# Second pair one batch at a time, and loads in a gated order, in a feature-map attention with an MLP

## The chip, the cores and the metric

The kernel runs on one core of a Trainium2 chip. A core has five engines with an instruction queue each, which run in order and wait for each other by semaphores: PE (TensorE, matmuls; its weight loads are shown as PEld), DVE (VectorE), ACT (ScalarE), POOL (GpSimd) and SP (SyncE, which here only issues DMAs). Sixteen DMA engines move the data. PE reads its operands from SBUF, the on-chip memory, and writes to PSUM, which has eight banks. The metric is the device time of one execution in microseconds (us), as the median of several runs. A profile of one execution gives the details.

## The reference

Attention with a feature map in place of the softmax, for 8 batches of 8 heads, 576 tokens, 64 channels per head and 128 features; then a layer norm and an MLP with a residual on the 512 joined channels.

```python
def phi(x):
    proj = einsum('bhsd,df->bhsf', x, w_phi)
    proj = proj - max(abs(proj), axis=-1, keepdims=True)
    return concatenate([exp(proj), exp(-proj)], axis=-1)
q_p, k_p = phi(q), phi(k)
kv  = einsum('bhsf,bhsd->bhfd', k_p, v)
z   = sum(k_p, axis=2)
num = einsum('bhsf,bhfd->bhsd', q_p, kv)
den = einsum('bhsf,bhf->bhs', q_p, z)[..., None] + 1e-06
x   = (num / den), heads joined: (8, 576, 512)
xn  = (x - mu) / sqrt(var + 1e-06) * g_ln
out = x + maximum(xn @ w_ch1, 0.0) @ w_ch2          # 512 -> 2048 -> 512
```

All of it is given and returned in float32. The kernel multiplies in bfloat16 and accumulates in float32.

## The kernel before, in words

The eight batches are worked in four pairs (`NPAIR`). One unit is two heads of 576 tokens; a pair has 8 units, so there are 32, numbered n = 0 to 31. A unit's 1152 token rows are eight full tiles of 128 rows and one mixed tile with the last 64 rows of both heads. `heads` says which two heads form a unit. In pair 0 they are two neighbouring heads of one batch, so that units 0 to 3 finish batch 0 and units 4 to 7 batch 1. In pairs 1 to 3 they are the same head of both batches, so that neither batch is finished before the eighth unit is.

**Steps of a unit.** The keys and queries are turned so that channels lie on partitions: on PE in pair 0 (`a_trans`, L485 and L493), and by a cast (`a_trans_dma`, L545 on DVE, L547 on ACT or L549 on POOL) and a transposing DMA on SP (L568) from unit 8 on. `a_mixed` (L590 to L607) treats the mixed tile. `a_k` multiplies the keys with `w_phi` (L632), takes the maxima on DVE (L638), the exponentials on ACT (L648), and scales the values on POOL into `vv` (`scale_main`, L659, L664 and L668). `a_q` and `a_tails` (units 0 to 3, L708 and L751) or `a_qt` (later units, L784 and L789) do the same for the queries, in both layouts. `a_kv` (L838, L843) sums key features times values over all tokens; `a_num` (L887, L893) multiplies with the query features, and DVE (L902, L907, L911) and POOL (L917) divide and put the result into `x`. In pair 0 each half unit's result goes to `x` in two pieces per head, and the mixed rows of the other half go through a buffer `xs` and a small DMA (L976).

**The MLP.** `x_stats` and `x_center` (L1034, L1049, L1053 or L1058) prepare the norm of each tile of `x`; the centered tiles are turned on PE in pair 0 (`x_trans`, L997) and by DMA later (`x_trans_dma`, L1021). `BLOCKS` groups the nine tiles of a pair: (0,2), (2,4), (4,6), (6,9) in pair 0, and three blocks of three tiles in the others. `moe_block` multiplies a block with `w1` (L1120, 16 groups of four matmuls), applies the ReLU on DVE or ACT (L1128, L1130), multiplies the previous block with `w2` (L1150), and adds `x` (L1157) before the store (L1082, L1091). Pair 0 has `g_ln` folded in when `x` is turned; from pair 1 on it is folded into `w1`, which DVE scales in place (`scale_w1`, L467, 16 operations) when pair 1's first block is due.

**Loads.** One DMA on SP brings one operand of one unit (256 KB), `load_tails` the mixed rows of four units in two DMAs of 64 KB. The order is: batch 0's, then those of units 4 and 5, 6 and 7, and later ones at their due times. `w1` (four blocks of 1 MB in float32, cast on the way) is issued by POOL (L440) once the second query has come, and `w2` (L451) once all of `w1` has.

**The order of the work.** No engine's order is written by hand. Every step is added to the class `Order` with its engines, an estimated time, what it reads and writes, the PSUM banks it takes (pool A: 2, B: 3, N: 1) and a rank. `backward` gives each step a latest start, counted back from the MLP's due times; to it an offset is added, from the table `OFF`, by the kind of step and one of three ranges of units (0 to 3, 4 to 7, later: `stage_table`). `run` plays the engines forward and gives each free engine the ready step of lowest rank. Where the plan has PE idle before `WARM` (36 us of the plan), it inserts filler matmuls on a zero tile `wz` (L1347), to keep PE's clock up. Each engine then gets its steps in the planned order, and on the chip they only wait for semaphores. `RING` (60) is the amount of outstanding DMA above which the plan holds an issuing queue back. Steps marked `port` get longer in the plan while POOL is busy, by 1.0 us at most.

Of the kernel before, what the change touches and what calls it, by code (L numbers as in the profile page):

```python
# [17 lines left out]
def bcast(ap: bass.AP, dim: int, n: int) -> bass.AP:  # L18
# [9 lines left out]
OFF = (  # L28
    {
        "en": 0, "gln": 404.4, "k": 731.6, "k.copy": 69.4, "k.em": -232.2, "k.exp": 2503.5,  # L30
        "k.max": 95, "k.trans": 40.9, "kv": 899.6, "kv.copy": -103, "ln": 482.7, "mixed": 18.6,
        "mixed.exp": -123.6, "mixed.max": 174.2, "num0": -2477.8, "num0.dve": -58.1,
        "num0.put": 178.6, "num1": 209.2, "num1.dve": 318.7, "num1.put": -457.6, "q.copy": -276.1,
        "q.trans": -426.8, "q0": -1263.9, "q0.em": 149.7, "q0.max": 0, "q1": -821.5,
        "q1.em": -990.6, "q1.max": -13.6, "tails0": -719.9, "tails0.exp": -90.7, "tails1": -225.7,
        "tails1.exp": 0, "vv": 215.8, "w2": 3061.6, "x.copy": -132.9, "x.trans": -1573.1,
    },
    {
        "en": 1225.8, "k": -596.1, "k.copy": 123.9, "k.em": 639.7, "k.exp": 9.2, "k.max": 81.3,
        "k.trans": -90.1, "kv": 0, "kv.copy": -360, "ln": 262.7, "load": 0, "mixed": -1206,  # L40
        "mixed.exp": -223.1, "mixed.max": 1308.1, "num0": 517.5, "num0.dve": -73.3,
        "num0.put": 141.8, "num1": 67.4, "num1.dve": -802.1, "num1.put": 0, "q.copy": -784.4,
        "q.em": 5.6, "q.max": 36.6, "q.trans": 753.5, "qt": -360.9, "rstd": -179.5,
        "tails.exp": 199, "vv": 2452.3, "x.copy": 195.6, "x.trans": -942.9,
    },
    {
        "en": 167.8, "k": 108.9, "k.em": 424.2, "k.exp": -788, "k.max": 25.2, "kv": -30.9,
        "kv.copy": 8.3, "ln": 12.2, "load": 1357.4, "mixed": -2096, "mixed.exp": 54.6,
        "mixed.max": 4.8, "num0": -162.6, "num0.dve": -161.9, "num0.put": -15.2, "num1": -692.4,
        "num1.dve": -457.5, "num1.put": -223.9, "q.em": -210.7, "q.max": -16.1, "qt": -860.5,  # L50
        "rstd": 81.2, "tails.exp": -53.9, "trans": 253.4, "vv": 2822.4, "w1": 1149.9,
    },
)
# [9 lines left out]
class Order:  # L63

    ENGINES = ("PE", "DVE", "ACT", "POOL", "SP")
    START, LAND, RING, TURN, COLD = 1.15, 0.75, 60.0, 0.095, 5.5
# [36 lines left out]
    def run(self):  # L103
# [21 lines left out]
        while True:  # L125
# [30 lines left out]
            for engine in self.ENGINES:  # L156
# [4 lines left out]
                while queue:  # L161
                    item = heapq.heappop(queue)
                    op = item[2]
                    if op.engine:
                        op = None
                        continue
                    full = op.dma and out.get(op.dma[0], 0.0) > self.RING
                    if not full and all(room[res] >= n for res, n in op.acquire):
                        break
                    passed.append(item)  # L170
                    op = None
# [18 lines left out]
                elif engine == "DVE" and op.port:  # L190
                    us += min(max(free["POOL"] - now, 0.0), 1.0)
# [22 lines left out]
def kernel(  # L214
# [44 lines left out]
    EARLY, NUMB, TILED = 4, 0, 4  # L259
# [40 lines left out]
    for i in range(2):  # L300
# [3 lines left out]
        nc.gpsimd.memset(vx, 0.0)  # L304
        nc.gpsimd.memset(vx[0:64, :, 0, D:D1], 1.0)
        nc.gpsimd.memset(vx[64:128, :, 1, D:D1], 1.0)
# [7 lines left out]
    for i in range(EXB):  # L314
        ex = consts.tile([P, 2, 2 * P], BF16, name=f"ex{i}")
        nc.gpsimd.memset(ex, 0.0)
        ex_bufs.append(ex)

    w1_sb = consts.tile([P, KC, DH], BF16, name="w1")
    w2_sb = consts.tile([P, JC, DM], BF16, name="w2")  # L320

# [40 lines left out]
    def issue(queue, rank, dst, src, keys, nbytes, row=1024):  # L362
        eng = nc.sync if queue == "SP" else nc.scalar
        dma(
            queue, rank, nbytes / row, lambda: eng.dma_start(out=dst, in_=src), w=keys,
            us=0.65 if row == 256 else 0.52, ns=0.019 if row == 256 else 0.045,
        )

    def heads(pair, i, half):

        if pair == 0:
            return i // 4, 2 * (i % 4) + half, 2
        return 2 * pair + half, i, 1

    def load_main(key, n, nu, rank, queue):
# [7 lines left out]
        if pair == 0:  # L383
# [9 lines left out]
                262144 * nu,  # L393
            )
            return
        for half in range(2):
# [7 lines left out]
                [(key + str(half), g % NBUF, u) for u in us], 131072 * nu,  # L404
            )

    def load_tails(key, n, rank, queue):
# [4 lines left out]
        for half in range(2):  # L412
# [9 lines left out]
            issue(queue, rank, dst, src, [(key + "x" + str(half), j)], 16384 * TG, row=256)  # L422
# [25 lines left out]
    def load_w2(n, V):  # L448
# [9 lines left out]
        dma("POOL", V, 512, emit, r=[("w1 came", NW - 1)], w=[("w2", n)], us=0.75, ns=0.094)  # L458

    def scale_w1(n, rank):  # L460
# [5 lines left out]
        def scale(kc):  # L466
            nc.vector.tensor_scalar(  # L467
                out=w1_sb[:, kc, sl], in0=w1_sb[:, kc, sl], scalar1=gln_sb[:, kc : kc + 1],
                scalar2=-1.0, op0=ALU.mult, op1=ALU.mult,
            )  # L470

        for kc in range(KC):
            add("DVE", 0.3, rank, lambda kc=kc: scale(kc), r=["gln"], w=[("w1", n, kc)])
# [63 lines left out]
    def a_trans_dma(u):  # L537
# [28 lines left out]
        def turn():  # L566
# [6 lines left out]
        add(("DVE", "ACT", "POOL"), (0.12, 0.19, 0.8), rank, cast_mixed,  # L573
# [5 lines left out]
            us=1.3, ns=0.019)  # L579

    def a_mixed(u):
# [11 lines left out]
        def maxima():  # L593
            nc.vector.reduce_max(
                out=u["m"][:, :, u["mx"]],
# [28 lines left out]
    def a_k(u):  # L624
# [17 lines left out]
        def em():  # L642
            t_ = u["em", 1]
            e = u["mx"] + 1
# [7 lines left out]
        def en():  # L652
            e = u["mx"] + 1
            nc.scalar.activation(u["en"][:, 0:e], u["m"][:, 1, 0:e], AF.Exp, scale=-1.0)

        def scale_main(t):
            vb, vx = v_bufs[u["g"] % NBUF], vx_bufs[n // TG % 2]
# [5 lines left out]
            )  # L663
            nc.gpsimd.tensor_copy(  # L664
# [5 lines left out]
                in1=bcast(bcast(e[:, u["mx"] : u["mx"] + 1], 1, 2), 3, D1), op=ALU.mult,  # L670
# [14 lines left out]
        for t, e in ((1, ("em", 1, n % NEM)), (0, ("en", n % NEM))):  # L685
            add("POOL", 1.5, rk("vv", n), lambda t=t: scale_main(t),
                r=[e, *vdata] + [("vv", 1, n % VVB)] * (1 - t), w=[("vv", t, n % VVB)])

    def q_part(u, s):

        qT = u["qkT"][:, 0:512]
        if s is None:
            return qT.rearrange("p (c t) -> p c t", t=P)
        return qT.rearrange("p (h s t) -> p s h t", h=2, s=2)[:, s]

    def a_q(u, s=None):

        n = u["n"]
        x = "" if s is None else str(s)
        nc_ = 4 if s is None else 2  # L700

        def products():
            shape = [P, 2 * nc_, F]
            pool, tag = (ps_A, "A") if s is None else (ps_B, "B")
            u["pq", s] = ps = pool.tile(shape, FP32, tag=tag, name="pq")
            chunks = q_part(u, s)
            for c in range(nc_):
# [4 lines left out]
        def maxima():  # L712
            m, ps = u["m"][:, 0, :], u["pq", s]
            if s is not None:
                out = m[:, 6 * s : 6 * s + 4]
            elif u["pair"]:
                out = m[:, 0:MX]
            else:
                out = m.rearrange("p (s r) -> p s r", s=2)[:, :, 0:4].rearrange(
                    "p s (h a) -> p h s a", h=2  # L720
                )
                ps = ps.rearrange("p (h s a) f -> p h s a f", h=2, s=2)
            nc.vector.reduce_max(out=out, in_=ps, axis=AX.X, apply_absolute_value=True)

        def em():
            lo, hi = {None: (0, u["mx"] + 1), 0: (0, 4), 1: (6, u["mx"] + 1)}[s]
# [4 lines left out]
        parts = (0, 1) if s is None else (s,)  # L731
        room = [("A" if s is None else "B", 1)]
        mk = [("m", 0, p, n % NEM) for p in parts]
        add("PE", mm(nc_, 256), rk("q" + x, n), products, r=[("qkT", n % QB, 0), ("T", n % QB, 0)],
            w=[("pq", s, n)], acquire=room)
# [649 lines left out]
```

## Time and profile before

| what | value |
|---|---|
| median of 6 runs | 385.44 us (383.11 to 386.6) |
| the profiled execution | 385.26 us |
| its span, first to last instruction | 383.5 us |
| mean granted PE clock | 0.989 |
| HBM read, written | 36.77 MB, 9.44 MB |
| DMA, mean over the span | 139 GB/s |
| PE's matmuls L1120, L1150 (the MLP), busy | 154.2 us, 144.5 us |
| PE's fillers L1347, busy | 24.1 us, x309 |

The profile gives, for each engine, the busy time and, for groups of instructions by line, the count, the mean duration and the idle time of the engine just before them with what ended it. Busy times of groups that overlap on PE add up to more than the engine's. A line of a timeline gives the start and the duration in us, the engine, the line of the kernel, the operation with its tiles, and in brackets the idle time before it. A line of windows gives a stretch of the run, its length, the busy time of PE, PEld, DVE, ACT and POOL with the number of instructions, the granted PE clock (1 is full), the DMA engines' busy share and the GB/s moved. Idle time of an engine that doesn't set the end costs nothing.

### The profile page before, as it was taken

To read this page: it belongs to the slowest core of one execution; us is meant where nothing else is said; L and a number is where in the kernel's file an instruction comes from. 1 tells how busy PE (TensorE), PEld (TensorE's weight loads), DVE (VectorE), ACT (ScalarE), POOL (GpSimd) and SP (SyncE) were. 2 spreads that over 40 slices of the span, in tenths; PEclk is the share of its full clock that TensorE was granted. 3 is DMA by queue.
4 is the path that set the end of the run, shared out by engine and by line. 5 is a ranking of instruction groups with operands and counts; after the bars stand their busy time and mean duration, and the time that the engine had idled before them with its cause. 6 is when DMAs were issued, how large, how long until landed. Compare 5 with 4: busy or idle time off the path is not lost.

```text
span 383.5 us, 9303 instructions
## 1 busy us (share of the span) xinstructions
PE 361.4 (94%) x3516; PEld 232.7 (61%) x3562; DVE 297.9 (78%) x633; ACT 226.5 (59%) x539; POOL 181.7 (47%) x334
## 2 busy tenths in 40 slices
PE   7999689998996999999999999999999999999995
PEld 6999567665763555656566656566665555555543
DVE  4789999996997899978987899788878745454532
ACT  3999997778975678786786777867643300000000
POOL 4958968976657666164655751654451000000000
PEclk9999999998998999999999999999999999999999
DMA  7999799799999674968452547310010530110102
GB/s 201 256 239 325 156 259 166 200 281 248 231 215 290 159 225 98 257 131 213 91 134 45 127 115 163 75 30 30 18 40 27 111 89 34 30 55 29 46 37 85
DMA packets 92589, 53.31 MB, mean 139 GB/s; under 512 B 59008, under 2 KB 88064, under 8 KB 92544
## 3 DMA queue, kind: packets, MB, share of 16 engines
q1 hardware_dynamic: 86944, 48.18, 49.3%
q0 software_dynamic: 4224, 4.19, 6.7%
q8 instruction: 28, 0.46, 0.5%
q10 hardware_dynamic: 1376, 0.33, 0.4%
q14 instruction: 17, 0.14, 0.1%
HBM read 36.77 MB, written 9.44 MB: 120 GB/s over the span
## 4 chain that ended last, share of the span: by engine, by line
PE 63%; DVE 12%; DMA 12%; POOL 6%; issue 3%; ACT 2%; SPq 1%; DVEq 0%; POOLq 0%; ACTq 0%
PE hT_ps L1120 25%; PE ch_ps L1150 23%; DMA qk<-in_k_dram 4%; PE n_bank L843 3%; DMA qkT<-b 3%; PE pk L632 2%; DVE w L467 2%; POOL vv L659 2%; PE n_bank L1347 2%; PE num L887 2%; DVE hT L1128 2%; DVE m L638 1%; PE pq L784 1%; POOL x L917 1%; DMA xT<-xc 1%
## 5 line engine op out<-in xcount | busy, mean ns | idle before, releaser
L1120 PE MATMUL hT_ps<-xT,w 128*128 128x384 bf16 (+1 forms) x832 | 154.2, 315 | 1.0 <-ACT xT L1009 0.3
L1150 PE MATMUL ch_ps<-w,hT 128*128 128x512 bf16 (+1 forms) x546 | 144.5, 376 | 4.0 <-ACT xT L1009 2.1
L1120 PEld LDWEIGHTS <-w 128*128 128x128 bf16 x832 | 77.8, 98 | 54.4 <-issue 4.9
L1128 DVE TENSOR_SCALAR hT<-hT_ps 128x384 bf16<-128x384 f32 (+1 forms) x136 | 71.4, 525 | 47.9 <-PE hT_ps L1120 46.0
L1150 PEld LDWEIGHTS <-hT 128*128 128x128 bf16 x592 | 54.7, 98 | 42.9 <-issue 3.7
L659 POOL TENSOR_TENSOR vv<-v,em 128x512 bf16<-128x512 f32 x64 | 67.7, 1058 | 24.4 <-ACT em L645 16.0
L917 POOL TENSOR_TENSOR x<-numc,rden 128x384 bf16<-128x384 f32 (+3 forms) x88 | 45.9, 536 | 66.5 <-DVE rden L911 64.5
L1130 ACT ACTIVATE hT<-hT_ps 128x384 bf16<-128x384 f32 (+1 forms) x72 | 33.3, 466 | 68.2 <-PE hT_ps L1120 67.8
L648 ACT ACTIVATE eb<-pk 128x1024 bf16<-128x1024 f32 x64 | 65.6, 1041 | 5.1 <-DVE m L638 5.0
L810 ACT ACTIVATE ea<-pt 128x1024 bf16<-128x1024 f32 x56 | 57.0, 1028 | 15.6 <-PE pt L789 15.1
L638 DVE TENSOR_REDUCE m<-pk 128x8 f32<-128x1024 f32 x32 | 38.8, 1214 | 5.1 <-PE pk L632 5.0
L803 DVE TENSOR_REDUCE m<-pq 128x8 f32<-128x1024 f32 x28 | 33.9, 1210 | 1.0 <-PE pq L784 1.0
L1157 DVE SCALAR_TENSOR_TENSOR o<-ch_ps,rstd,x 128x512 f32<-128x512 f32 (+1 forms) x37 | 26.9, 728 | 9.1 <-PE ch_ps L1150 7.9
L887 PEld LDWEIGHTS <-ea 128*128 128x128 bf16 x512 | 25.6, 99 | 8.0 <-issue 1.9
L843 PE MATMUL n_bank<-vv,eb 128*128 128x65 bf16 x512 | 26.9, 194 | 0.0
L843 PEld LDWEIGHTS <-eb 128*128 128x128 bf16 x512 | 22.3, 98 | 7.0 <-issue 4.1
L632 PE MATMUL pk<-wbk,qkT 128*128 128x256 bf16 x128 | 20.0, 281 | 6.7 <-DVE m L803 5.4
L549 POOL TENSOR_TENSOR b<-qk,one 128x1024 bf16<-128x1024 f32 x11 | 21.1, 1915 | 10.9 <-DMA qkT<-b 10.9
L668 POOL TENSOR_TENSOR vv<-vx,em 128x130 bf16<-128x130 f32 x64 | 26.1, 409 | 0.0
L1034 DVE BATCH_NORM_STATS2 st<-x 128x6 f32<-128x512 bf16 (+1 forms) x44 | 24.5, 582 | 0.7 <-POOL x L917 0.5
L1347 PE MATMUL n_bank<-wz 128*128 128x120 bf16 x309 | 24.1, 229 | 0.4 <-DVE KV L850 0.4
L902 DVE TENSOR_TENSOR numc<-num,em 128x390 f32<-128x390 f32 (+2 forms) x40 | 20.6, 514 | 1.7 <-PE num L887 0.5
(89 smaller groups left out, 446.3 us busy)
## 6 DMA issues: line engine op xcount, KB each, us to landing
qk<-in_k_dram SPq DMA_DIRECT2D x32, 256.0 KB, 4.0
v<-in_v_dram SPq DMA_DIRECT2D x32, 256.0 KB, 3.8
qk<-in_q_dram SPq DMA_DIRECT2D x32, 256.0 KB, 5.1
out_dram<-o SPq DMA_DIRECT2D x31, 256.0 KB, 2.6
w<-in_moe_w_ch_dram POOLq DMA_DIRECT2D x8, 512.0 KB, 9.3
out_dram<-o SPq DMA_DIRECT2D x9, 128.0 KB, 2.5
qx<-in_k_dram SPq DMA_DIRECT2D x16, 64.0 KB, 4.2
vx<-in_v_dram SPq DMA_DIRECT2D x16, 64.0 KB, 3.8
```

The costliest lines, as they stand in the source:

```text
L638: nc.vector.reduce_max(out=u["m"][:, 1, 0:MX], in_=u["pk"], axis=AX.X, apply_absolute_value=True)
L648: nc.scalar.activation(u["EB"][:, t, 0:MX, :], u["pk"], AF.Exp, scale=(1.0, -1.0)[t])
L659: nc.gpsimd.tensor_tensor(out=u["vv"][:, t, 0:MX, 0:D], in0=vb[:, hh, :].rearrange("p (c d) -> p c d", d=D), in1=bcast(e[:, 0:MX], 2, D), ...
L803: nc.vector.reduce_max(out=out, in_=ps, axis=AX.X, apply_absolute_value=True)
L810: nc.scalar.activation(u["EA"][:, t, :], u["pt", None], AF.Exp, scale=(1.0, -1.0)[t])
L843: nc.tensor.matmul(ps[:, t, c // 4, :], EB[:, t, c, :], vv[:, t, c, :], start=False, stop=(t == 0 and c == MX - 1), skip_group_check=True,)
L887: nc.tensor.matmul(ps[t][:, i, :], ea(u, t, c), KV[:, t, c // 4, :], start=True, stop=True,)
L917: nc.gpsimd.tensor_tensor(out=dst, in0=st["numc"][ps_, i : i + n, 0:D], in1=bcast(st["rden"][ps_, i : i + n], 2, D), op=ALU.mult,)
L1120: nc.tensor.matmul(st["ps"], w1_sb[:, kc, jj * P : (jj + 1) * P], xT_bufs[xj][:, kc : nt * KC : KC, :], start=(kc == 0), stop=(kc == KC - 1),)
L1128: nc.vector.tensor_relu(h_sb[:, 0 : nt * P], st["ps"])
L1130: nc.scalar.activation(h_sb[:, 0 : nt * P], st["ps"], AF.Relu)
L1150: nc.tensor.matmul(ch[t, c][:, cols], hT[jj][:, rt * P : (rt + 1) * P], w2_sb[:, jj, cols], start=(jj == 0), stop=(jj == JC - 1),)
```

## The change

- **Pair 1 by batches.** `SPLIT = 2`: units 8 to 11 are batch 2 and units 12 to 15 batch 3, as in pair 0. The query maxima now lie in tile order, without gaps. `a_num` puts a unit's result in two pieces per head in pair 1 too, and its mixed rows go through `xs`. `x_stats` works on half rows for pair 1's full tiles. `BLOCKS` is unchanged, so pair 1's first block (tiles 0 to 2) needs batch 2 alone, the second (tiles 3 to 5) both batches.
- **Loads.** SP gets two gates, tiny DMAs that read a piece of a weight block and so wait for it: one on the third block of `w1`, ahead of batch 1's loads, and one on the third block of `w2`, ahead of all loads from unit 8 on. `w2` waits for the query of unit 7 to have come (before: for the last block of `w1`). Units 8 to 15 are loaded two at a time, 512 KB in one DMA.
- **Memsets.** Those of the `vx` and `ex` buffers move from POOL to DVE.
- **vv in two steps.** The scaling of the full tiles no longer waits for the mixed rows; these and the column of ones are a step of their own on POOL.
- **scale_w1** multiplies with the negated scale alone and may run on DVE or ACT.
- **The order model.** `RING` is 128 and counts the DMA to be issued; DVE's wait for POOL has no upper limit; some estimates change; `OFF` has a value for each of the units 0 to 11, for units 12 to 15 and for each later pair. All engines' orders are new.

```diff
-    START, LAND, RING, TURN, COLD = 1.15, 0.75, 60.0, 0.095, 5.5
+    START, LAND, RING, TURN, COLD = 1.15, 0.75, 128.0, 0.095, 5.5
...
-                    full = op.dma and out.get(op.dma[0], 0.0) > self.RING
+                    full = op.dma and out.get(op.dma[0], 0.0) + op.dma[1] > self.RING
...
-                    us += min(max(free["POOL"] - now, 0.0), 1.0)
+                    us += max(free["POOL"] - now, 0.0)
...
-    EARLY, NUMB, TILED = 4, 0, 4
+    EARLY, SPLIT, GATE = 4, 2, 2
...
-        nc.gpsimd.memset(vx, 0.0)
-        nc.gpsimd.memset(vx[0:64, :, 0, D:D1], 1.0)
-        nc.gpsimd.memset(vx[64:128, :, 1, D:D1], 1.0)
+        nc.vector.memset(vx, 0.0)
+        nc.vector.memset(vx[0:64, :, 0, D:D1], 1.0)
+        nc.vector.memset(vx[64:128, :, 1, D:D1], 1.0)
...
-        nc.gpsimd.memset(ex, 0.0)
+        nc.vector.memset(ex, 0.0)
...
+    def gate_of(n):
+        return None if n < H // 2 else "w1" if n < H else "w2"
+
+    def gate(key, n):
+        src = w1_sb[0:1, 0, n * WC : n * WC + 8] if key == "w1" else w2_sb[0:1, n * JC // NW, 0:8]
+        add(
+            "SP", 0.6, rk("load", 0), lambda: nc.sync.dma_start(out=seen, in_=src),
+            r=[("w1", n, 0) if key == "w1" else ("w2", n)], w=[("gate", key)], lag=0.0,
+        )
+
     def heads(pair, i, half):
-        if pair == 0:
-            return i // 4, 2 * (i % 4) + half, 2
+        if pair < SPLIT:
+            return 2 * pair + i // 4, 2 * (i % 4) + half, 2
         return 2 * pair + half, i, 1
...
-        dma("POOL", V, 512, emit, r=[("w1 came", NW - 1)], w=[("w2", n)], us=0.75, ns=0.094)
+        dma("POOL", V, 512, emit, r=gate, w=[("w2", n)], us=0.75, ns=0.094)
...
-        def scale(kc):
-            nc.vector.tensor_scalar(
-                out=w1_sb[:, kc, sl], in0=w1_sb[:, kc, sl], scalar1=gln_sb[:, kc : kc + 1],
-                scalar2=-1.0, op0=ALU.mult, op1=ALU.mult,
-            )
+        def scale(kc, engine):
+            w, g = w1_sb[:, kc, sl], ngln[:, kc : kc + 1]
+            if engine == "DVE":
+                nc.vector.tensor_scalar_mul(out=w, in0=w, scalar1=g)
+            else:
+                nc.scalar.activation(w, w, AF.Copy, scale=g)
...
-            add("POOL", 1.5, rk("vv", n), lambda t=t: scale_main(t),
-                r=[e, *vdata] + [("vv", 1, n % VVB)] * (1 - t), w=[("vv", t, n % VVB)])
+            add("POOL", 1.0, rk("vv", n), lambda t=t: scale_main(t),
+                r=[e, *vdata[0:2]] + [("vv", 1, n % VVB)] * (1 - t), w=[("vv", t, n % VVB)])
+            add("POOL", 0.5, rk("vv", n), lambda t=t: scale_rest(t),
+                r=[e, *vdata[2:4]] + [("vvx", 1, n % VVB)] * (1 - t), w=[("vvx", t, n % VVB)])
...
-        if pair:
+        if not split:
             h = u["h"]
...
-            t0, ht = 4 * b + 2 * part, 2
+            ht = min(nt, MX - lo) // 2
+            t0 = 4 * b + lo // 2
...
-        split = pair == 0 and t < MX
+        split = pair < SPLIT and t < MX
...
-        return (n >= H // 2) + (n >= H)
+        return n if n < 12 else 11 + n // 8
...
-    add("POOL", 4.6, -999.0, None)
+    add("POOL", 1.8, -999.0, None)
-    add("DVE", 1.3, -999.0, None)
+    add("DVE", 3.0, -999.0, None)
...
-    for key in "kqv":
-        load_tails(key, 4, next(rank), "SP")
+    gate("w1", NW - 2)
     for n in (4, 5):
-        for key in "kvq":
-            load_main(key, n, 1, next(rank), "SP")
-    for n in range(NW):
-        load_w2(n, rk("w2", 0))
+        if n == 4:
+            for key in "kqv":
+                load_main(key, 4, 1, next(rank), "SP")
+                load_tails(key, 4, next(rank), "SP")
+        else:
+            for key in "kvq":
+                load_main(key, n, 1, next(rank), "SP")
...
+            if n == 1:
+                for j in range(NW):
+                    load_w2(j, rk("w2", 0), [("came", "q", 7)])
+                gate("w2", GATE)
...
-            if w["pair"] == 0:
+            if w["pair"] < SPLIT:
                 tiles = range(4) if i < 4 else range(4, NT)
```

## The prediction

> **What bounds the kernel now.** I read the page's part 1, then stretches of the run, then the waits of PE, then the start on DVE and POOL. Part 1 (busy us, share of the span, instructions):
>
> ```profile
> PE 361.4 (94%) x3516; PEld 232.7 (61%) x3562; DVE 297.9 (78%) x633; ACT 226.5 (59%) x539; POOL 181.7 (47%) x334
> ```
>
> PE sets the time. Its 94% hides 24.1 us of warm-up fillers (L1347 x309, all before 39 us). Stretches in us from the start, with busy time of each engine, PE clock, DMA share, GB/s:
>
> ```profile
> 10.00:40.00 30.00, 29.25 (x540) 27.99 (x538) 25.17 (x56) 27.60 (x77) 23.26 (x50) 1.00 1.11 279
> 40.00:65.00 25.00, 20.65 (x278) 15.90 (x277) 23.75 (x58) 22.08 (x56) 21.64 (x45) 1.00 0.98 189
> 65.00:100.00 35.00, 32.55 (x352) 22.28 (x357) 30.88 (x75) 29.24 (x74) 24.21 (x46) 0.95 0.93 227
> 100.00:134.00 34.00, 29.25 (x313) 19.61 (x316) 29.77 (x55) 23.08 (x55) 24.48 (x38) 0.95 0.98 230
> 134.00:160.00 26.00, 24.83 (x228) 14.11 (x230) 25.91 (x61) 19.90 (x47) 13.88 (x21) 1.00 0.72 185
> 160.00:300.00 140.00, 138.51 (x1326) 83.54 (x1347) 119.31 (x250) 98.87 (x225) 69.71 (x121) 1.00 0.39 93
> ```
>
> From 160 us to the end of the matmuls at 375.6 us PE is full, and no reordering there can help. All that can be won lies before 160 us: from 40 to 160 us PE idles 4.35 + 2.45 + 4.75 + 1.17 = 12.7 us. Two waits are long (start, us, operation, the idle time before it in brackets):
>
> ```profile
> 87.73 0.67 PE L1150 MATMUL ch_ps<-w,hT 128*128 128x512 bf16 x2 [2.08 <-ACT xT L1009]
> ...
> 122.58 1.01 PE L632 MATMUL pk<-wbk,qkT 128*128 128x256 bf16 x4 [3.69 <-DVE m L803]
> ```
>
> Each is followed by half-speed matmuls:
>
> ```profile
> 88.00:90.00 2.00, 2.00 (x16) 1.32 (x15) 0.62 (x2) 1.92 (x8) 1.12 (x1) 0.53 0.61 175
> 90.00:92.00 2.00, 2.00 (x9) 0.96 (x8) 1.11 (x6) 1.97 (x6) 1.70 (x3) 0.62 1.37 235
> ...
> 122.00:124.00 2.00, 1.42 (x6) 0.84 (x6) 2.00 (x5) 0.43 (x3) 2.00 (x4) 0.56 0.99 322
> 124.00:126.00 2.00, 2.00 (x21) 1.27 (x19) 1.45 (x2) 0.57 (x4) 1.22 (x1) 0.58 1.06 364
> ```
>
> The clock column gives 2 x (0.47 + 0.38) = 1.7 us lost after the first and 2 x (0.44 + 0.42) = 1.7 us after the second. The second wait stands behind L467 (x16, 676 ns) on DVE. The start on DVE, where the fillers' operand wz comes early, and on POOL:
>
> ```profile
> 1.15 0.11 DVE L1343 MEMSET wz<- 128x64 uint32 x1
> 3.83 1.64 DVE L289 CAST wbk<-wphi_f 64x128 bf16<-64x128 f32 x2 [2.58 <-DMA wphi_f<-in_w_phi_dram]
> 5.49 0.23 DVE L331 CAST wst<-wphi_f 128x128 bf16<-128x128 f32 x1
> ```
> ```profile
> 3.24 1.92 POOL L316 MEMSET ex<- 128x512 bf16 x4
> ```
>
> **What the Trainium skill says.** "TensorE: Matmul & The Clock Gate", section "What's actually happening": after an idle window of about 3.4 us the array runs at half clock, until a whole busy window has passed. The trace agrees in kind: 0.53 to 0.62 for some 4 us after each long wait. "SBUF — State Buffer", section "SBUF: two separate sides": GpSimd and a VectorE operation of a two-port mode exclude each other for whole instructions. The trace agrees: the 64x128 casts took 814 ns beside POOL's memsets, the larger wst cast 227 ns without them. "DMA: Bandwidth & Descriptors", section "Queues, rings and completion order": one issuing engine's descriptors are consumed in ring order, so a late small transfer stands behind earlier bulk. The trace agrees: a key load issued at 20.52 us, with a dozen before it, took 14.34 us, against a median of 4.0.
>
> **The change part by part.** Positions below come from the instruction order of both built kernels.
>
> Start. Nine memsets move from POOL to DVE, and in the built order DVE makes wz only after them, both wbk casts, wst and the m memsets. DVE's own memsets give about 0.06 us plus 0.83 ns an element (wbk: 128 in 165 ns). Two of 520 cost 1.0, four small 0.3, five of 256 words 1.35. With the casts free of POOL (some 0.2 each) and wphi landing at 3.7 to 4.0, wz is ready near 5.9 us, where it was 1.26. PE runs 19 fillers at 105 ns before its first transpose, so this starts near 8 us instead of 3.62. That is 4.5 us late. It isn't all lost: from first to last filler, PE's real work ahead of the last filler is 14.5 us against 15.3 before, and 10 fillers are gone. At full clock the two sequences are 30.0 and 31.2 us. Before ran its half-clock part until 9.67 us, 3.85 us into its sequence. After starts at 5.9 and warms near 10.5, some 2.3 us in; 10.5 + 27.7 = 38.2 us, and 38.7 before. So the fillers absorb the delay, but 0.8 us less work is done, and ACT and DVE start 3 to 4 us later, for which I add 1.2: minus 2 us.
>
> First MLP block. Before, the first L1120 matmul stands at 46.8 us. After, the four units of batch 0 are finished first and their MLP matmuls follow the last filler, near 40 us. DVE has some 28 us of work from 8.5 us to this point, so it can't be much earlier. Between 40 and 65 us PE idled 4.35 us; with MLP work to put between the attention steps I take nearly all: plus 4.
>
> The two long waits. At unit 12 before had issued 192 of its MLP matmuls (136 L1120, 56 L1150); after has 236 and 84. When unit 15's keys are due it has 260 and 144 against 220 and 76. The w1 scaling becomes 5 DVE and 11 ACT operations, in a one-scalar form: 16 x 0.676 = 10.8 us of DVE become about 5 x 0.49 (L1053's row) plus 11 x 0.72 on ACT (L1058's row), on an engine with 10 us free in this stretch. I take both waits and their slow clock: 2.1 + 3.7 + 3.4 = plus 9.2. The smaller waits of 65 to 160 us (2.6 us) I leave.
>
> Loads. Batch 0 is unchanged until its last query. SP then waits at a gate until the third w1 block has come, and everything behind it on SP (batch 1, the small move into x, the stores) waits too. A weight block costs 6.7% of the 383.5 us over 8 blocks, 3.2 us. With w1 begun near 15.3 us behind 2 us of batch 0, the third lands near 27; batch 1 (ten loads of 256 KB and six of 64 KB up to its last query, 3.0 MB, at the 340 GB/s of 30 to 40 us) has it by 40 us. Unit 4's keys come at 30 instead of 24.3, still before PE's place for them near 31. POOL's four w2 issues (0.8 us each) wait for that query and hold vv of unit 4 behind them until 46 us; PE has 44 L1120 matmuls before it needs that. w2's third block opens the second gate near 52 us. Behind it stand, on SP, 6.55 MB of loads and two stores, and only then the transposes of units 8 and 9. One w2 block (3.2) and 7.1 MB at 340 GB/s (21) end near 76 us, and the transpose takes 3.6: 80 us. At the 250 GB/s of mixed traffic it is 28 and 87 us. PE reaches unit 8's queries after 38 us of work from 40 us, so at 78 to 80. I take a wait of 3 us and 1 of slow clock: minus 4, with ends 0 and minus 13.
>
> Batch by batch in pair 1. Its first MLP block (three tiles, near 21 us of PE) is free after unit 11 rather than 15. The price: POOL makes 120 output multiplies instead of 96, about 7 us over units 8 to 15, hidden under POOL's 30% of idle time from 65 to 160 us; DVE makes 52 statistics instead of 44, some 1.5 us. But from unit 8 to 16 PE has near 60 us to do and DVE near 59, so neither waits for the other without loss: minus 2.
>
> The later part (units 16 to 31, tail of 7.9 us after the last matmul) has the same work: 0. The split of vv into two steps and the costs in the order model add no work: 0; if POOL's cover fails, vv costs up to 0.4 us a unit.
>
> Sum: -2 + 4 + 9.2 - 4 - 2 = 5.2 us. The composition adds about 2: with more MLP and fewer units done at the same time, DVE is a few us less behind at unit 8, and that stretch is nearer PE's own work. 7.2 us off the span of 383.5 is 376.3. The profiled run took 385.26, 1.8 more than its span, close to the median of 385.44. So 378.2 us.
>
> **Rivals.**
> 1. The second gate starves unit 8 (slower). At 250 GB/s its transposes land near 87 us, PE stands 9 us plus 2 of slow clock, and ACT and DVE dry up, which delays units 9 to 11 by another 2. That is 13 instead of 4: 9 us worse, near 387. It decides when the wait there passes about 11 us. For it: 227 to 230 GB/s in 65 to 134 us. Against: pure loads reached 340.
> 2. Waits only move. The new order has stalls of its own as long as the old two; 13.2 us won is lost at other places: 384 to 386.
> 3. Full gain: loads at 340 GB/s, no loss at unit 8, small waits gone too: 5.2 + 4 + 2 + 2.6 + 2 = 16 us, near 370.
> That the reordering does nothing is excluded: no engine's queue keeps its order.
>
> **How the numbers follow.** Forecast (374 to 383) 0.44, full gain 0.20, waits only move 0.12, starved 0.24. 0.5% is 1.9 us, about what a measurement here can tell. Faster: 0.44 + 0.20 + a little of rival 2, 0.66; within it 0.10; slower 0.24. The range, 369 to 390, takes in the full gain and most of the starved case; the forecast's own is 374 to 383.
>
> **What would show it.** First PE matmul near 6 us; first MLP matmul near 40; a gap of PE before unit 8's queries between 77 and 88 us; no clock below 0.9 from 118 to 130 us; PE full from about 90 us. I'm wrong if PE's real work at 100 us is no more than before, or if waits over 2 us appear between 100 and 160 us.

## The result, and the profile after

The changed kernel takes 384.74 us (median of 28 runs, 379.64 to 388.57); the kernel before, on the same chips, 384.33 us (63 runs). The ratio is 0.9978, with a 95% interval of 0.9957 to 0.9999. It is the ratio of the fast runs alone (17 of the 28): runs over 1.5% above the fastest of their kernel are left out, and so it lies below the 1.001 of the two medians. The forecast was 378.2 us, 7.2 below the 385.44 of the six earlier runs. The profiled execution of the changed kernel took 383.35 us with a span of 381.6, where that of before had 385.26 and 383.5: 1.9 us less, about as little as the ratio says. What came is the rival called "waits only move", which had 0.12.

Part 1 of the page after (busy us, share of the span, instructions) looks like that of before: 2.3 us less PE work, of which 1.1 are warm-up fillers.

```profile
PE 359.1 (94%) x3513; PEld 231.0 (61%) x3552; DVE 294.3 (77%) x645; ACT 228.6 (60%) x543; POOL 187.9 (49%) x358
```

The stretches of the kernel after, with the same columns as in the prediction (length, busy time of PE, PEld, DVE, ACT and POOL, PE clock, DMA share, GB/s):

```profile
0.00:10.00 10.00, 3.99 (x41) 3.97 (x42) 4.21 (x26) 1.39 (x2) 0.70 (x6) 1.00 0.76 205
10.00:40.00 30.00, 27.71 (x503) 26.00 (x500) 23.35 (x55) 26.45 (x78) 22.84 (x47) 1.00 0.82 185
40.00:65.00 25.00, 20.96 (x220) 15.85 (x222) 16.96 (x39) 15.71 (x42) 11.84 (x26) 0.86 0.92 197
65.00:100.00 35.00, 34.27 (x360) 24.44 (x362) 32.46 (x80) 25.48 (x59) 21.37 (x45) 1.00 1.04 261
100.00:134.00 34.00, 32.74 (x327) 19.75 (x332) 31.45 (x66) 28.89 (x63) 25.10 (x55) 1.00 0.74 196
134.00:160.00 26.00, 24.71 (x271) 15.61 (x270) 23.40 (x53) 21.72 (x54) 20.20 (x39) 1.00 0.99 215
160.00:300.00 140.00, 138.60 (x1396) 84.48 (x1413) 120.60 (x249) 102.33 (x238) 85.38 (x144) 1.00 0.45 106
```

The gain is where it was forecast. From 65 to 160 us PE idles 0.73 + 1.26 + 1.29 = 3.3 us instead of 8.4, and the clock is 1.00 where two stretches had 0.95; with the 3.4 us of slow clock, some 8.5 us are won. The longest wait of PE that is left there is 1.0 us. The four slices that showed the slow clock before are now at full clock:

```profile
88.00:90.00 2.00, 2.00 (x24) 1.11 (x21) 1.79 (x4) 0.93 (x3) 0.40 (x1) 1.00 1.34 144
90.00:92.00 2.00, 2.00 (x24) 1.67 (x21) 1.99 (x4) 2.00 (x4) 1.36 (x1) 1.00 0.81 207
122.00:124.00 2.00, 2.00 (x19) 0.98 (x18) 2.00 (x5) 2.00 (x6) 1.85 (x6) 1.00 0.94 316
124.00:126.00 2.00, 1.86 (x25) 1.11 (x25) 1.72 (x4) 2.00 (x8) 1.92 (x5) 1.00 0.89 233
```

It is spent ahead of that. The first 10 us hold 3.5 us less PE work than before, the next 30 us 1.5 less (before: 29.25). From 40 to 65 us PE is busy for as long as before, but at a clock of 0.86, and DVE, ACT and POOL lose 6 to 10 us of work each (before: 23.75, 22.08, 21.64). The first 10 us of the kernel before:

```profile
0.00:10.00 10.00, 7.51 (x70) 6.81 (x71) 4.66 (x17) 3.38 (x10) 4.49 (x18) 1.00 0.75 202
```

The start is as predicted; on DVE of the kernel after (start, us, operation, idle time before it in brackets) and on PE:

```profile
4.66 0.82 DVE L445 MEMSET ex<- 128x256 uint32 x3
5.49 0.23 DVE L462 CAST wst<-wphi_f 128x128 bf16<-128x128 f32 x1
5.67 0.21 DVE L477 MEMSET m<- 128x24 f32 x5
5.84 0.11 DVE L1473 MEMSET wz<- 128x64 uint32 x1
```
```profile
6.01 0.28 PE L1474 MATMUL n_bank<-wz 128*128 128x120 bf16 x1 [6.01 <-DVE wz L1473]
```

The hole at 40 us is not where the prediction looked for one. PE stands there again and again for keys and queries of batch 1 (PE in order of time, kernel after):

```profile
40.01 0.40 PE L632 MATMUL qkT_ps<-ident,qk 128*128 128x128 bf16 x4 [1.00 <-DMA qk<-in_k_dram]
...
45.01 0.40 PE L632 MATMUL qkT_ps<-ident,qk 128*128 128x128 bf16 x4 [1.96 <-DMA qk<-in_q_dram]
...
47.08 0.54 PE L632 MATMUL qkT_ps<-ident,qk 128*128 128x128 bf16 x4 [0.80 <-DMA qk<-in_k_dram]
...
49.33 0.61 PE L632 MATMUL qkT_ps<-ident,qk 128*128 128x128 bf16 x4 [0.86 <-DMA qk<-in_k_dram]
```

No wait is longer than 2 us, but after this row of them the clock is 0.50 from 48 to 54 us:

```profile
42.00:44.00 2.00, 0.68 (x7) 0.23 (x5) 0.91 (x4) 0.77 (x2) 0.00 (x0) 1.00 1.15 230
...
48.00:50.00 2.00, 1.14 (x9) 0.61 (x7) 0.19 (x1) 0.84 (x5) 0.78 (x1) 0.50 1.17 247
50.00:52.00 2.00, 2.00 (x13) 1.45 (x12) 0.32 (x1) 1.73 (x3) 2.00 (x6) 0.50 1.17 246
52.00:54.00 2.00, 2.00 (x12) 1.39 (x10) 1.14 (x4) 2.00 (x4) 1.85 (x6) 0.50 1.18 244
```

Why the keys are late is seen on SP and POOL. SP has issued its last load of batch 0 by 11.0 us, stands 17.6 us in front of the first gate (POOL issues w1 only from 17.00 us on), and then puts batch 1 out one transfer at a time up to 41.9 us. POOL meanwhile issues all four blocks of w2 (SP's waits; SP and POOL in order of time; all of the kernel after):

```profile
SPq L507 <- DMA w<-in_moe_w_ch_dram: 17.6, 1, 17.6
```
```profile
28.72 0.81 SPq L507 DMA_DIRECT2D seen<-w  x1
29.59 0.39 SPq L496 DMA_DIRECT2D qk<-in_k_dram  x1
...
39.81 0.71 SPq L496 DMA_DIRECT2D qk<-in_q_dram  x1
40.61 1.25 SPq L496 DMA_DIRECT2D v<-in_v_dram  x2
```
```profile
37.79 3.04 POOL L596 DMA_DIRECT2D w<-in_moe_w_ch_dram  x4
```

With SP at its gate and w1 not yet issued, the DMA engines run dry: they move 94, 0 and 59 GB/s in the three slices from 14 to 20 us, where without the first gate (the last experiments) they move 339, 216 and 159. The middle slice of the kernel after:

```profile
16.00:18.00 2.00, 2.00 (x37) 1.84 (x34) 1.04 (x3) 2.00 (x7) 2.00 (x4) 1.00 0.00 0
```

The load at 39.81 us is unit 7's query, the one that w2 was planned to wait for (`r=gate` with `("came", "q", 7)`). POOL has issued the first block two microseconds earlier. The key is a dependency in the order model only: w2's transfer touches nothing of the query, so no semaphore came of it. The gates on SP do wait, since they are transfers that read the weights. The blocks of w2 and the loads of batch 1 then share the DMA engines, at 230 to 247 GB/s, until w2's last block has landed at 57.6 us. "DMA: Bandwidth & Descriptors" of the Trainium skill, section "Queues, rings and completion order", says that a DMA engine goes round robin between the queues that have work for it; the trace agrees: unit 6's and 7's keys, issued at 38.78 us and just after, took 8 and 10 us, and w2's first block 8.4, where it takes 5.8 when no loads of batch 1 are under way (the kernel without the first gate, below).

Theory when the experiments began: the gain is paid away by two things, the late start, which the fillers don't absorb, and w2 meeting batch 1's loads. The experiments moved the cause one step further back.

### The profile page after: what moved, and what is told of

Same layout as the page of the kernel before. It is cut to its first block, busy times and chain, and to the rows that moved or that the text cites. A ratio compares the mean times of both kernels' runs of the same rounds, so it can differ in the third digit from the quotient of the medians.

```text
span 381.6 us, 9301 instructions
## 1 busy us (share of the span) xinstructions
PE 359.1 (94%) x3513; PEld 231.0 (61%) x3552; DVE 294.3 (77%) x645; ACT 228.6 (60%) x543; POOL 187.9 (49%) x358
## 4 chain that ended last, share of the span: by engine, by line
PE 75%; DMA 11%; ACT 4%; DVE 3%; issue 3%; SPq 2%; POOL 1%; ACTq 0%; DVEq 0%
PE hT_ps L1251 29%; PE ch_ps L1281 24%; DMA qkT<-b 5%; PE n_bank L1477 4%; PE n_bank L975 3%; PE pk L779 3%; DMA qk<-in_k_dram 3%; PE num L1018 3%; PE pq L918 2%; DMA xT<-xc 2%; ACT eb L795 1%; PE pt L923 1%; SPq L496 1%; PE n_bank L970 1%; ACT ea L942 1%
## 5 line engine op out<-in xcount | busy, mean ns | idle before, releaser
L1251 PE MATMUL hT_ps<-xT,w 128*128 128x384 bf16 (+1 forms) x832 | 152.5, 317 | 1.1 <-DMA xT<-xc 1.0
L1281 PE MATMUL ch_ps<-w,hT 128*128 128x512 bf16 (+1 forms) x553 | 141.0, 373 | 1.9 <-issue 0.2
L1259 DVE TENSOR_SCALAR hT<-hT_ps 128x384 bf16<-128x384 f32 (+1 forms) x143 | 74.9, 527 | 49.5 <-PE hT_ps L1251 47.9
L1047 POOL TENSOR_TENSOR x<-numc,rden 128x192 bf16<-128x192 f32 (+4 forms) x112 | 49.6, 460 | 53.3 <-DVE rden L1041 45.0
L1261 ACT ACTIVATE hT<-hT_ps 128x384 bf16<-128x384 f32 (+1 forms) x65 | 29.5, 462 | 55.7 <-PE hT_ps L1251 55.3
L696 POOL TENSOR_TENSOR b<-qk,one 128x1024 bf16<-128x1024 f32 x14 | 26.5, 1892 | 11.2 <-DMA qkT<-b 9.9
L1165 DVE BATCH_NORM_STATS2 st<-x 128x6 f32<-128x256 bf16 (+1 forms) x52 | 24.9, 512 | 1.1 <-POOL x L1047 0.9
L1477 PE MATMUL n_bank<-wz 128*128 128x120 bf16 x299 | 23.0, 225 | 0.8 <-ACT KV L984 0.5
L1032 DVE TENSOR_TENSOR numc<-num,em 128x390 f32<-128x390 f32 (+2 forms) x36 | 19.2, 534 | 2.7 <-PE num L1018 1.8
L1477 PEld LDWEIGHTS <-wz 128*128 128x128 bf16 x299 | 19.1, 103 | 1.4 <-issue 1.1
```

The lines of the kernel that those rows point to most:

```text
L1047: nc.gpsimd.tensor_tensor(out=dst, in0=st["numc"][ps_, at, 0:D], in1=bcast(st["rden"][ps_, at], 2, D), op=ALU.mult,)
L1251: nc.tensor.matmul(st["ps"], w1_sb[:, kc, jj * P : (jj + 1) * P], xT_bufs[xj][:, kc : nt * KC : KC, :], start=(kc == 0), stop=(kc == KC - 1),)
L1259: nc.vector.tensor_relu(h_sb[:, 0 : nt * P], st["ps"])
L1281: nc.tensor.matmul(ch[t, c][:, cols], hT[jj][:, rt * P : (rt + 1) * P], w2_sb[:, jj, cols], start=(jj == 0), stop=(jj == JC - 1),)
L1477: nc.tensor.matmul(warm, wz, wz[:, 0:WN], start=False, stop=False, skip_group_check=True)
```

## The experiments

All times below are medians beside runs of the kernel before on the same chip. A difference between two changed kernels is taken between their ratios, and 1% is 3.84 us; the intervals of two ratios are added in quadrature.

**w2 made to wait.** One small copy on POOL reads unit 7's query ahead of w2's first issue.

```diff
+    seen_q = consts.tile([P, 8], FP32, name="seen_q")
 ...
+            if n == 0:
+                nc.gpsimd.tensor_copy(out=seen_q, in_=qk_bufs[0][:, 0, 1, 0:8])
```

> The kernel after, in the same order on every engine, with one small POOL copy ahead of the four w2 issues that reads unit 7's query, so that w2 really starts only once that query is in. Theory A (in the kernel after w2 shares the DMA engines with batch 1's loads, and PE waits for keys and queries from 38 to 50 us, 6 us in all, and then runs some 7 us at half clock): batch 1's last query lands near 43 us instead of after 50, PE's idle time from 40 to 50 us falls from 4.0 to below 1 us, no half clock, 5 to 7 us faster than after, ratio to before 0.980 to 0.986. Theory B (the volume of data before unit 8 sets the pace): the same bytes come in another order, PE waits for w2 or for unit 8 instead, ratio 0.994 to 1.000.

Measured: 380.13 us, ratio 0.9877 [0.9832, 0.9922], so 1.0% or 3.9 us below the kernel after (2.0 to 5.8). POOL issues w2 at 44.35 us; unit 7's keys land at 45.3 instead of 49.3; the stretch from 40 to 65 us has its clock back and 2.7 us more PE work in this kernel:

```profile
40.00:65.00 25.00, 23.67 (x289) 18.11 (x288) 22.30 (x54) 21.71 (x55) 19.37 (x42) 1.00 1.00 219
```

So w2's meeting with batch 1 costs. The ratio lies between the two theories, nearer to A: some of the gain is lost again in a new wait of 4.0 us before xT_ps (L1131), with a clock of 0.90 from 65 to 100 us.

**wz made first on DVE.** The memset stands ahead of the others; all else is as after.

```diff
+    wz = consts.tile([P, P], BF16, name="wz")
+    nc.vector.memset(wz, 0.0)
     wphi_f = ...
```

> The kernel after, in the same order, with the zero tile of the fillers made first on DVE. Theory A (as predicted, the fillers absorb the late start): first matmul near 1.2 us instead of 6.0, PE's filler phase ends at the same time near 41 us because it waits for loads there, at most 1 us faster than after, ratio 0.995 to 0.999. Theory B (what PE lost from 0 to 10 us, 3.5 us against before, is lost at the end): 3 to 4 us faster than after, ratio 0.987 to 0.991.

Measured: 380.09 us, ratio 0.9858 [0.9801, 0.9914]: 1.2% or 4.6 us (2.3 to 6.9) below the kernel after. This is a little beyond theory B. Read alone, it says that the late start costs twice what the prediction took. The runs without gates, below, show that it is not the start as such.

**Both mends.** The two diffs together: w2 made to wait, and wz first.

> Both edits. Theory A of the first and A of the second: ratio 0.979 to 0.985, little better than w2 waiting alone. If with batch 1's data in time the start decides when the first MLP block begins: 2 to 4 us better than w2 waiting alone, ratio 0.972 to 0.980.

Measured: 376.54 us, ratio 0.9793 [0.9753, 0.9834]; the two savings add up within their intervals, 1.85% or 7.1 us for 8.5 us taken singly. This is about the forecast. With PE begun at 1.0 us, POOL issues w1 at 14.29 us instead of 17.00, and the gate opens at 25.72 instead of 28.72. An earlier start means an earlier gate: the two mends may be two ways around one thing.

**The one-scalar scaling in the kernel before.**

```diff
-            nc.vector.tensor_scalar(
-                out=w1_sb[:, kc, sl], in0=w1_sb[:, kc, sl], scalar1=gln_sb[:, kc : kc + 1],
-                scalar2=-1.0, op0=ALU.mult, op1=ALU.mult,
+            nc.vector.tensor_scalar_mul(
+                out=w1_sb[:, kc, sl], in0=w1_sb[:, kc, sl], scalar1=ngln[:, kc : kc + 1]
             )
```

> The kernel before, in the same order, with w1 scaled by one scalar (the negated one) instead of two, all still on DVE. Theory A (the 3.69 us wait of PE at 122.58 us stands behind these operations): one takes 0.26 to 0.49 us instead of 0.676, the wait falls below 1.5 us and the half clock after it goes, 3 to 5 us faster, ratio 0.987 to 0.992. Theory B (DVE is full there anyway and POOL holds the shared port): less than 1 us, ratio 0.997 to 1.000.

Measured: 384.06 us, ratio 0.9981 [0.9950, 1.0011]. The operation keeps its cost (mean 676 ns in both forms, 319 to 1129 and 320 to 1129), which is theory B. In the profile the wait of 3.69 us is 2.48, and the clock after it is 1.00. But this profiled execution took 382.27 us and that of the kernel before 385.26, where the medians don't differ: executions of one kernel differ by as much. Of the 100 executions of the kernel before that ran beside the experiments, the 17 with a mean clock of 0.998 or more took 381.3 to 383.3 us, and the 22 with 0.989, as in its profile, 385.1 on average. So the shorter wait and the full clock in this trace can't be put down to the edit, and a wait in one profile is not worth its length.

**Both mends, no gates.** The gate stays in the plan and issues nothing.

```diff
-            "SP", 0.6, rk("load", 0), lambda: nc.sync.dma_start(out=seen, in_=src),
+            "SP", 0.6, rk("load", 0), lambda: None,
```

> The kernel with both mends (wz first, w2 behind unit 7's query), with neither gate on SP: the two 16-byte moves are gone, every other instruction stands in the same order. It was 376.5 us with the gates. Theory A, the gates are not what costs: the first keeps batch 1 off the DMA engines while w1 comes, the second has nothing late behind it; without them w1's third block lands later than 28 us, some of the first 40 us moves about, and the time is 376 to 379. Rival B, the gates hold up SP for nothing: units 4 to 7 get their keys up to 6 us earlier, the key and query waits at 38 to 44 us (some 3 us of PE) are gone, and the time is 371 to 374.

Measured: 373.87 us, ratio 0.9746 [0.9715, 0.9777]; 0.5% below the kernel with both mends and its gates, with an interval that just reaches no difference. The time is at the upper end of B's band, and of the key and query waits 0.4 us is left (2.3 with the gates). It has the lowest median of the study.

**Both mends, the first gate only.**

```diff
+            "SP", 0.6, rk("load", 0), lambda: key == "w1" and nc.sync.dma_start(out=seen, in_=src),
```

> The kernel with both mends, with the first gate kept and the second gate taken out: SP issues unit 8's and 9's loads without waiting for w2's third block. It was 376.5 us with both gates. Theory A: nothing on PE waits for unit 8's transposes, so the second gate is free, and the time is 375.5 to 377.5. Rival B, the second gate starves unit 8: its keys' products, at 87.5 us with the gate, come 3 us or more earlier, and the time is below 374. Rival C, the second gate protects w2: without it w2 shares the DMA engines with unit 8's loads, the first product of the second MLP layer (52.0 us) comes 3 us or more later, and the time is above 378.5.

Measured: 374.85 us, ratio 0.9785 [0.9748, 0.9823], not to be told from both gates (0.9793). Unit 8's keys' products come at 87.0 us, with the second gate at 87.5, and w2 is not late (first product of the second layer at 51.8 and 52.0 us). Here the second gate neither starves unit 8 nor protects w2. The median is 0.7 us under theory A's band; the ratio is in line with it.

**The memsets on DVE, alone, in the kernel before.**

```diff
-        nc.gpsimd.memset(vx, 0.0)
+        nc.vector.memset(vx, 0.0)
 ...
-        nc.gpsimd.memset(ex, 0.0)
+        nc.vector.memset(ex, 0.0)
```

> The kernel before with one part of the change alone: the vx and ex memsets made by DVE instead of POOL; DVE then makes wz last of all, after the memsets, the casts and the m buffers, as in the kernel after. Theory A, the late start is a loss of its own that the fillers don't give back: first matmul near 6 us, PE does some 3.5 us less in the first 10 us, and the time is 387 to 389 (ratio 1.007 to 1.012). Rival B, as the prediction had it, the fillers absorb most of the delay: last filler as before near 38.7 us, time 384 to 386.5 (1.000 to 1.005). Rival C, the memsets help here too, since wbk's casts no longer run beside POOL: below 384.

Measured: 385.71 us, ratio 1.0048 [1.0027, 1.0069]: 1.8 us slower, 1.0 to 2.7. First matmul at 5.9 us, last filler at 40.3 us instead of 38.5. The first 10 us lose 3.4 us of PE work, as in the kernel after, but about half of it is given back later (first two stretches of this kernel):

```profile
0.00:10.00 10.00, 4.13 (x40) 3.92 (x41) 4.05 (x24) 1.28 (x1) 0.70 (x6) 1.00 0.74 201
10.00:40.00 30.00, 29.58 (x538) 28.45 (x537) 24.73 (x53) 27.89 (x79) 21.46 (x47) 1.00 1.07 253
```

The time is in rival B's band, the prediction's own price, though the last filler comes 1.8 us later and not as before. From 10 to 40 us PE does as much as before (29.58 for 29.25), where the kernel after does 27.71. So the late start by itself doesn't cost work from 10 to 40 us. On DVE the two wbk casts take 0.22 us each with POOL's memsets gone; beside them they took 0.81 (kernel before).

**Pair 1 as before the change, with both mends.** SPLIT is 1; the order is planned anew, with offsets that were chosen for SPLIT 2.

```diff
-    EARLY, SPLIT, GATE = 4, 2, 2
+    EARLY, SPLIT, GATE = 4, 1, 2
```

> The kernel with both mends, with pair 1 done as before the change, both batches of a head at a time (SPLIT 1 instead of 2), so that pair 1's first MLP block is free after unit 15 rather than 11; the order is planned anew with the same table of offsets, which was not chosen for it. It was 376.5 us. Theory A, batch by batch is what keeps PE fed at units 8 to 15: waits of over 2 us come back between 100 and 160 us, and the time is 379 to 384. Rival B, batch 0's MLP work, begun 6 us earlier, and w2 in time are enough: no such waits, POOL has 24 multiplies less, and the time is 374 to 378.

Measured: 408.70 us, ratio 1.0634. PE waits 6.0 us at once and the clock is 0.74 from 134 to 160 us. This is far beyond both theories, and no measure of batch by batch: with a table of offsets that doesn't fit, the order itself is bad. What batch by batch is worth stays open.

**The kernel after, no gates.** Neither mend; the edit is that of the run with both mends and no gates.

> The kernel after with neither gate on SP; every other instruction in the same order. It was 384.7 us with the gates (ratio 0.998 to the kernel before). Theory A: the gates cost it 2 to 3 us, as the middle values of the two mended kernels with and without them say (376.5 and 373.9): SP's loads for units 4 to 7 start earlier, fewer of them meet w2, the key and query waits at 38 to 50 us shrink, and the time is 379 to 382.5. Rival B: the gates matter only once the start and w2 are mended, and the time is 383 to 386. Rival C: without the first gate w1, w2 and batch 1 all share the DMA engines from 17 us on, and the time is above 386.

Measured: 375.83 us, ratio 0.9754 [0.9698, 0.9811]: 2.2% or 8.6 us below the kernel after. All three theories missed it. Taking the two gates out brings about as much as the two mends together (2.2% and 1.85%, not to be told apart), and without gates the mends bring nothing more that shows (0.9746 with them, 0.9754 without; up to 0.7% either way is not excluded). So most of what the start and w2's missing wait cost the kernel after, they cost because of the gates.

**The scaling of w1 all on DVE.** In the kernel after, the eight scalings that the plan gave to ACT run on DVE at the same places of the order.

```diff
-            if engine == "DVE":
+            if True:
                 nc.vector.tensor_scalar_mul(out=w, in0=w, scalar1=g)
```

> The kernel after with the eight scalings of w1 that the plan gave to ACT put on DVE, at the same places of the order; all 16 then run on DVE in the one-scalar form, as in the kernel before apart from the form. It was 384.7 us. Theory A, as the prediction's third step has it, the relief of DVE is part of what removed the two long waits: DVE gets some 4.5 us more between 107 and 128 us, PE has a wait of 2 us or more there, and the time is 386 to 389. Rival B, the rebuilt order has slack enough at that place: no wait over 1 us in 100 to 134 us, and the time is 384 to 386.

Measured: 385.94 us, ratio 1.0041 [1.0013, 1.0070], 0.6% or 2.4 us (1.0 to 3.8) above the kernel after. From 100 to 134 us PE is busy 31.59 us instead of 32.74, with one wait for DVE that the kernel after doesn't have (waits of PE in this stretch: us in total, times, longest):

```profile
PE n_bank L1018 <- DVE KV L982: 1.7, 1, 1.7
```

The time is at the upper end of rival B's band, the wait between the two theories (2 us or more, none over 1). As the time is above that of the kernel after, beyond the interval, relief of DVE is a part of what keeps PE fed there.

**One gate at a time, in the kernel after.** Without the first:

```diff
+            "SP", 0.6, rk("load", 0), lambda: key == "w2" and nc.sync.dma_start(out=seen, in_=src),
```

> The kernel after without its first gate (the one behind w1's third block) and with its second. With neither it took 375.8 us, with both 384.7. Theory A, the first gate alone is what costs: SP issues batch 1's loads in 18 to 27 us as without gates, all of them land before 40 us, w2 then has the DMA engines to itself, no half clock at 46 to 54 us, and the time is 376 to 378.5. Rival B, the cost is shared between both gates: 379 to 382. Rival C, the second gate is the costly one: above 382.

And without the second (`key == "w1"` in the same line):

> The kernel after without its second gate (the one behind w2's third block) and with its first. Theory A, the first gate alone costs: batch 1 still meets w2 at 38 to 56 us, the half clock at 46 to 54 us stays, SP waits for the move into x until 59 us anyway, and the time is 383 to 385. Rival B, shared: 379 to 382. Rival C, the second gate is the costly one, since it holds back unit 8's loads: 376 to 379.

Measured: without the first gate 375.60 us, ratio 0.9779 [0.9740, 0.9818], which is 2.0% or 7.6 us below the kernel after (5.9 to 9.3). Without the second 382.95 us, ratio 0.9957 [0.9933, 0.9980], which is 0.8 us below the kernel after (-0.4 to 2.0) and not to be told from it. Both are theory A's readings, each a little under its band (by 0.4 and 0.05 us). So it is the first gate that costs. Without the second gate the stretch from 40 to 65 us keeps its slow clock:

```profile
40.00:65.00 25.00, 18.37 (x200) 14.08 (x201) 16.00 (x37) 14.91 (x39) 10.59 (x23) 0.86 0.89 185
```

The kernel without the first gate, on SP and in stretches:

```profile
16.65 1.26 SPq L496 DMA_DIRECT2D vx<-in_v_dram  x2
17.96 0.60 SPq L496 DMA_DIRECT2D qk<-in_k_dram  x1
...
24.13 5.41 SPq L496 DMA_DIRECT2D v<-in_v_dram  x2
```
```profile
10.00:40.00 30.00, 29.23 (x535) 27.83 (x533) 24.24 (x59) 27.08 (x80) 22.91 (x47) 1.00 1.03 244
40.00:65.00 25.00, 24.78 (x314) 19.43 (x312) 23.36 (x54) 22.98 (x53) 19.68 (x42) 1.00 0.88 188
```

SP is through with batch 1 at 29.5 us instead of 41.9, and the DMA engines move 244 GB/s from 10 to 40 us instead of 185: that difference over 30 us is 1.8 MB that the gate put off. Batch 1's last load lands at 39.1 us, and POOL issues w2 at 37.74 us into DMA engines that are nearly free (290 GB/s from 36 to 38 us, 34 from 38 to 40). w2 still doesn't wait for the query; it has nothing to meet. From 40 to 65 us PE is full, at full clock. The price of leaving out the gate is that w1's last block lands at 37.1 us instead of 31.2. The first MLP matmul comes at 40.7 us, 3.6 us later.

The run with w2 made to wait keeps the gate and gets half of this back (0.9877). So by the middle values the meeting with w2 is about half of the gate's cost, or more, since that run pays for its new wait of 4.0 us; the rest would be batch 1's lateness itself, which no run took alone.

## Why the prediction was wrong

**Start, minus 2: right.** The first matmul came at 6.01 us, and the same edit in the kernel before costs 1.8 us. In the kernel without the first gate the first 40 us hold 33.5 us of PE work against 36.8 before; 1.1 of the difference are fillers, so 2.2 us are lost, and the last filler is at 39.7 us. Once the gates are gone, making wz first (with w2 made to wait) brings nothing that the intervals, 0.6% together, can show.

**First MLP block, plus 4: right but for the gate.** The forecast was near 40 us; it came at 45.2, since PE stood for batch 1's keys and queries ahead of it. Without the first gate it comes at 40.7 us, and 40 to 65 us holds 24.78 us of PE work against 20.65 before: plus 4.1.

**The two long waits, plus 9.2: right in the traces,** which show some 8.5 us. These are two single executions, and 3.4 us of it is slow clock, which not every execution of the kernel before has (17 of 100 had a mean clock of 0.998 or more); in the median the gain is not measured apart. The details were off: the plan gave 8 scalings to each engine, not 5 and 11, and on DVE one took 559 ns, not 490. Putting the eight back costs 2.4 us.

**Loads, minus 4: this step failed,** in its place and its size. It let the first gate pass with the words that batch 1 has its last query by 40 us, "at the 340 GB/s of 30 to 40 us". That rate was measured before with loads already queued. The gate opened at 28.7 us, not near 27, since w1 was issued at 17.00 us and not near 15.3. Behind it SP has 18 loads to put out, 12.3 us of issuing (29.6 to 41.9 us), and the slices from 30 to 38 us moved 142 to 203 GB/s at a DMA share of 0.48 to 0.79, where the full ones from 44 to 52 us have 1.17: SP's issuing bounds it, not the DMA engines. The last query was not there at 40 us; it was only issued at 39.8. Even with w2 out of its way it landed at 43.9 (the run with w2 made to wait).

The same step then let w2 wait for this query, which the order model does and the engines don't. What the step feared, a gap before unit 8 behind the second gate, didn't come: unit 8's transposes landed at 88.6 us and its keys' products stand at 92.5, but PE had MLP work and idled 0.73 us from 65 to 100. No cost of the second gate shows (0.8 us, -0.4 to 2.0). The first gate costs 7.6 us (5.9 to 9.3), by the traces at 30 to 55 us, where the prediction had booked nothing. The forecast was a saving of 7.2 us, and the measured ratio is one of 0.8: of the 6.4 us between them this step is 3.6 (7.6 for 4), and the other steps together, below, are the rest.

**Batch by batch, minus 2, and composition, plus 2:** not measured. With the first gate away the whole change is worth 2.2% or 8.5 us (0.9779; 7.0 to 10.0), where the prediction's steps other than the loads add up to 11.2. So together these steps were some 3 us too high, and which of them is not shown.

**Rivals.** "The second gate starves unit 8" looked for the loss behind a gate, but behind the wrong one of the two. "Waits only move" was what the time did; its place, the loads at 40 us, had not been named. Of the signs to look for, no clock below 0.9 from 118 to 130 us and no long wait from 100 to 160 us held; the first MLP matmul near 40 us and the gap at 77 to 88 us did not, and the first of these was the one that told. The prediction's own sign of being wrong came too: up to 100 us PE is busy for 63.9 us with work other than fillers, against 65.9 before (68.1 without the first gate).

## What to carry to other kernels

A wait put on a queue holds everything behind it, and when it opens, the queue must still issue that work one transfer at a time; count the issues behind a gate, and don't price them by a rate that the trace shows for a full queue. Before a gate is put in to protect a transfer, ask when that transfer is needed: here w1 had 3.6 us to spare without it. And a dependency in a planner is a wait only if it becomes a semaphore; check in the trace that the releaser comes before the released.

## What was not expected of the hardware

- The array went to half clock with no long wait. From 42 to 50 us PE was idle for 4.0 of 8 us in pieces of at most 2.0 us, and the clock was 0.50 from 48 to 54 us. "TensorE: Matmul & The Clock Gate" of the Trainium skill, sections "What's actually happening" and "HAM oscillation — how this bites in real kernels", speaks of an idle gap of over some 3.4 us. Here a row of short ones was enough. Nor does the length of a single wait decide in these traces: a wait of 2.08 us was followed by 0.53 to 0.62 (kernel before, at 87.73 us), while after one of 2.48 us (the one-scalar run), and after 2.5 us of idle time in pieces (kernel before, 40 to 46 us), the clock stayed at 1.00. What decides is not shown.
